# Attention in steps of a pair of heads, planned together with two networks

## The chip, the cores and the metric

One core of one Trainium2 chip runs the whole program. The metric is the device time of one execution in microseconds (us), the median over several. TensorE (PE) multiplies; VectorE (DVE), ScalarE (ACT) and GpSimd (POOL) do the elementwise work; SyncE (SP) issues most DMAs. PE reads its operands from SBUF and writes to PSUM, which has eight banks of 512 fp32 columns.

## What is computed

Attention over 4 batches and 8 heads of 64: 512 local queries see the keys within 32 positions and 32 global keys; 32 global queries see all 544 keys. Its outputs, 4 × 544 rows of 512, go through two networks of width 2048.

```python
def _attn_ref(q_l, k_l, v_l, q_g, k_g, v_g):
    ...
    s_g = scale * np.matmul(q_g, k_all.transpose(0, 1, 3, 2))
    out_g = np.matmul(sm(s_g), v_all)
    ...
    mask = np.abs(pos[:, None] - pos[None, :]) <= window
    s_ll = np.where(mask, s_ll, -1000000000.0)
    s_lg = scale * np.matmul(q_l, k_g.transpose(0, 1, 3, 2))
    a_l = sm(np.concatenate([s_lg, s_ll], axis=-1))
    out_l = np.matmul(a_l, np.concatenate([v_g, v_l], axis=2))
    return np.concatenate([out_g, out_l], axis=2)

def _moe_ref(x, w_in, w_out):
    h = x @ w_in
    return (h * np.cos(h)) @ w_out

def _moe2_ref(x, w_in, w_out):
    h = np.maximum(x @ w_in, 0.0)
    return h * h @ w_out
```

## The kernel before, in words

**Two parts.** Attention comes first and leaves its output, transposed, in `xt`. Then the networks run: each product of a network is made of seven products of half blocks (sums of blocks in, sums of blocks out), in fp32 split into a high and a low part (`split`), in 48 steps. The `ha`, `he`, `hb` products (line 848) are the first layers, `y` (line 940) the second. Weights and x must be split before their products. A planner arranges the networks: each piece of work is an `Op` with a cost on each engine that may do it, with what it needs, and with a latest due time worked back from its users; it places always the piece that can start first, by due time.

**Attention's items.** It runs in 40 items: 32 `Local(p, hb)`, each half of the 512 queries of a pair p of heads, and 8 `Global(b, g)`, each the global queries of four heads. A group is two pairs, so four local items, and one global item; there are eight. A local item does:

- `s_mm` (line 400): scores of four blocks of 64 queries against 160 keys (128 in the window and 32 global), as eight 64 by 64 products; two heads lie in the row halves, two query blocks in the column halves of the array.
- `softmax`: on DVE mask and minimum into `pt`, with the minimum into `st` (line 416), then the exponential on ACT (426). `recip`: sum and reciprocal on DVE (440, 444). `norm`: the global keys' part into `pg` on POOL (449), four blocks of 128 keys, two on DVE (458), two on POOL (463).
- `t_mm` (469, 470): transposes of the probabilities; `t_evac` (475, 479): copies by ACT into `tws` and `tgs`.
- `o_mm`: for each of two query blocks the product of global keys (line 485) at full height, the values `VGZ` padded with zeros to 128 rows, then the window's values (497, `VA` and `VB`, which is `VA` shifted by 64 rows by DMA). `o_evac` copies to `xt` (510).

A global item has the same steps (527 scores, 542 maxima, 551 exponential, 572 normalization, 580 and 583 transposes, 599 values).

**Keys and queries.** `load_k` brings a group's keys so that the 32 global keys stand first: five DMAs a group; the last 32 local keys are left over and are loaded for each batch by themselves (`ktail`). `tr_k` (295) transposes, `k_evac` copies with ACT (308), `k_copy` has POOL make the shifted windows (333) and copies of the global keys for each block (335), and `k_tail` adds the rest. `tr_q` (350) and a copy on DVE (356) do the same for queries.

**Order.** It is written by hand: a table says for each kind of step how many items it lags, and in which order the steps of one round are issued; `BG`, `CB` and `CC` are places in that round where pieces of background (splits of weights and x for the first products) are put by number. Each engine takes its instructions in that order.

```python
CFG = {'order': ['CV', 'LQ', 'S', 'TE', 'BG', 'LK', 'OM', 'TRK', 'KEV', 'CC', 'SM',
           'RC', 'NM', 'CB', 'LV', 'OE', 'TRQ', 'QE', 'KC', 'TM'],
```

Here the minima (`SM`) of an item stand ahead of the reciprocal (`RC`, lag 1) of the item before it. PSUM banks: 0 and 1 transposes, 2 `tg`, 3 to 5 scores, 6 and 7 outputs. After the last item the networks are issued as planned, and `first`, `early` and `late`, the memory of attention, are given up one by one.

## Time and profile before

| what | value |
|---|---|
| time, median of 3 runs | 868.71 us (868.68 to 869.48) |
| the profiled execution: time, span | 867.5 us, 865.7 us |
| PE, DVE, ACT, POOL busy, share of the span | 98%, 75%, 61%, 66% |
| granted PE clock, mean | 1.00 |
| DMA | 182.00 MB, 210 GB/s |

Span is the time between the first and the last instruction of the trace. Busy times count what an engine executes, and not what it issues or waits for. In a timeline the first number is an instruction's start, the second its duration; consecutive instructions of one kind stand in one row with their number, and successive ones overlap, so the distance between starts is what one costs. A product in fp32 leaves two records.

### The profile page before, as it was taken

To read this page: it belongs to the slowest core of one execution; us is meant where nothing else is said; L and a number is where in the kernel's file an instruction comes from. 1 tells how busy PE (TensorE), PEld (TensorE's weight loads), DVE (VectorE), ACT (ScalarE), POOL (GpSimd) and SP (SyncE) were. 2 spreads that over 40 slices of the span, in tenths; PEclk is the share of its full clock that TensorE was granted. 3 is DMA by queue.
4 is the path that set the end of the run, shared out by engine and by line. 5 is a ranking of instruction groups with operands and counts; after the bars stand their busy time and mean duration, and the time that the engine had idled before them with its cause. 6 is when DMAs were issued, how large, how long until landed. Compare 5 with 4: busy or idle time off the path is not lost.

```text
span 865.7 us, 17214 instructions
## 1 busy us (share of the span) xinstructions
PE 847.4 (98%) x6028; PEld 782.1 (90%) x6028; DVE 650.4 (75%) x1521; ACT 529.5 (61%) x1275; POOL 571.1 (66%) x634
## 2 busy tenths in 40 slices
PE   7999999999999999999999999999999999999998
PEld 6777787999999999999999998889988989898886
DVE  7788897999798777967688899896756677454544
ACT  5789787987776666566555777555544554343331
POOL 5479886999797555757377999985635647441221
PEclk9999999999999999999999999999999999999999
DMA  7898865657694578546726646666764677446733
GB/s 165 207 206 183 176 206 185 243 176 247 231 363 154 178 269 312 177 164 266 304 84 227 248 169 240 220 233 237 264 222 140 239 281 231 134 161 246 221 116 84
DMA packets 134262, 182.00 MB, mean 210 GB/s; under 512 B 60960, under 2 KB 114720, under 8 KB 134176
## 3 DMA queue, kind: packets, MB, share of 16 engines
q1 hardware_dynamic: 130736, 179.79, 63.0%
q10 hardware_dynamic: 3440, 1.11, 0.5%
q8 instruction: 48, 0.79, 0.4%
q14 instruction: 38, 0.31, 0.1%
HBM read 141.03 MB, written 35.65 MB: 204 GB/s over the span
## 4 chain that ended last, share of the span: by engine, by line
PE 83%; POOL 4%; DMA 3%; ACT 3%; DVE 2%; SPq 2%; issue 1%; ACTq 0%; POOLq 0%
PE y L940 39%; PE hb L848 15%; PE he L848 10%; PE ha L848 10%; DMA vb<-va 2%; PE s L400 2%; PE o L485 2%; PE o L497 1%; POOL g L172 1%; POOL xs L172 1%; PE tw L469 1%; POOL wf L163 1%; DMA kn<-in_k_l_dram 1%; ACT pt L426 1%; PE tk L295 1%
## 5 line engine op out<-in xcount | busy, mean ns | idle before, releaser
L172 POOL TENSOR_TENSOR g<-cr,g 128x384 fp32r<-128x384 f32 (+1 forms) x192 | 202.6, 1068 | 146.0 <-ACT g L899 141.2
L951 DVE TENSOR_TENSOR xt<-y,xt 128x384 f32<-128x384 f32 (+2 forms) x287 | 170.4, 595 | 96.2 <-PE y L940 94.5
L940 PE MATMUL y<-g,wo 128*128 128x384 f32 (+1 forms) x1152 | 219.2, 327 | 0.4 <-DVE wo L172 0.3
L940 PE MATMUL y<-wo,g 128*128 128x512 f32 x816 | 209.4, 393 | 0.0
L940 PEld LDWEIGHTS y<-g,wo 128*128 128x128 f32 x1152 | 194.1, 188 | 1.5 <-DVE wo L172 0.5
L940 PEld LDWEIGHTS y<-wo,g 128*128 128x128 f32 x816 | 150.0, 188 | 24.1
L848 PE MATMUL hb<-xs,wi 128*128 128x384 f32 (+1 forms) x864 | 166.4, 327 | 1.4 <-ACT cr L888 1.2
L848 PEld LDWEIGHTS hb<-xs,wi 128*128 128x128 f32 x864 | 146.7, 188 | 7.7 <-ACT cr L888 1.6
L848 PE MATMUL he<-xs,wi 128*128 128x384 f32 (+1 forms) x576 | 111.0, 327 | 1.6 <-DVE cr L891 0.8
L848 PE MATMUL ha<-xs,wi 128*128 128x384 f32 (+1 forms) x576 | 110.9, 327 | 0.8 <-DVE cr L891 0.7
L899 ACT ACTIVATE g<-cr 128x384 fp32r<-128x384 f32 (+1 forms) x192 | 93.6, 500 | 20.6 <-DVE cr L891 19.5
L163 POOL TENSOR_TENSOR wf<-wf,cc 128x512 uint32<-128x512 uint32 x64 | 88.3, 1384 | 26.7 <-DVE wf L151 18.6
L848 PEld LDWEIGHTS he<-xs,wi 128*128 128x128 f32 x576 | 98.0, 188 | 6.2 <-DVE cr L891 1.5
L848 PEld LDWEIGHTS ha<-xs,wi 128*128 128x128 f32 x576 | 97.6, 188 | 3.5 <-DVE cr L891 1.0
L885 ACT ACTIVATE cr<-cr,halfpi 128x384 f32<-128x384 f32 (+1 forms) x96 | 55.9, 592 | 11.9 <-DVE cr L880 10.6
L156 DVE SCALAR_TENSOR_TENSOR cc<-raw,cc 128x512 uint32<-128x512 uint32 x64 | 60.9, 958 | 0.0
L426 ACT ACTIVATE pt<-pt,st 128x160 f32<-128x160 f32 x128 | 53.1, 425 | 0.5 <-DVE st L416 0.5
L856 ACT ACTIVATE s<-hb 128x384 f32<-128x384 f32 (+1 forms) x48 | 22.7, 473 | 48.5 <-PE hb L848 48.4
L147 ACT ACTIVATE cc<-raw 128x512 uint32<-128x512 uint32 x64 | 42.5, 670 | 15.9 <-DMA raw<-in_moe_w_in_dram 7.2
L151 DVE TENSOR_SCALAR wf<-wf 128x512 uint32<-128x512 uint32 x64 | 50.0, 785 | 2.7 <-POOL wf L142 1.7
L416 DVE CUSTOM_DVE_ANT_0 pt<-s,mask 128x160 f32<-128x160 f32 x128 | 33.8, 319 | 12.9 <-PE s L400 12.4
L856 ACT ACTIVATE s<-he 128x384 f32<-128x384 f32 (+1 forms) x48 | 22.6, 471 | 32.4 <-PE he L848 32.2
(147 smaller groups left out, 1322.1 us busy)
## 6 DMA issues: line engine op xcount, KB each, us to landing
xs<-xs_T SPq DMA_DIRECT2D x48, 768.0 KB, 5.6
xs<-xs_B SPq DMA_DIRECT2D x36, 768.0 KB, 5.2
raw<-in_moe_w_in_dram SPq DMA_DIRECT2D x32, 512.0 KB, 5.3
raw<-in_moe_w_out_dram SPq DMA_DIRECT2D x32, 512.0 KB, 4.7
xs<-xs_T SPq DMA_DIRECT2D x24, 640.0 KB, 5.6
xs_T<-xs SPq DMA_DIRECT2D x16, 768.0 KB, 4.0
xs<-xs_B SPq DMA_DIRECT2D x18, 640.0 KB, 5.0
xs_B<-xs SPq DMA_DIRECT2D x12, 768.0 KB, 4.8
```

The source lines that it names most:

```text
L147: A.activation(v, raw[q, m, c][:, :, 0].bitcast(U32), AF.Copy, scale=2.0**-29)
L151: V.tensor_scalar(u, u, 3, None, op0=ALU.logical_shift_left)
L156: V.scalar_tensor_tensor(v, t[:, :, 1].bitcast(U32), 0x80000000, v, op0=ALU.bitwise_and, op1=ALU.bitwise_or,)
L163: G.tensor_tensor(u, u, v, op=ALU.add)
L172: eng.tensor_tensor(lo, x, hi.bitcast(F32), op=ALU.subtract)
L426: nc.scalar.activation(self.pt[:, u, :], self.pt[:, u, :], AF.Exp, bias=self.st[:, 0, u : u + 1], scale=-1.0, accum_out=self.st[:, 1, u : ...
L848: nc.tensor.matmul(out, lhsT=w[:, ws, c : c + P], rhs=xs[:, xh, kk, 0:n], start=start and k == 0, stop=k == 5, skip_group_check=True,)
L856: A.activation(self.sb[name], self.hold(bank_name), AF.Copy)
L885: A.activation(self.r[key], self.r[key], AF.Sin, bias=halfpi, scale=TWOPI)
L899: A.activation(GT[s, f][0][:, th * n : th * n + n], self.r[key], AF.Copy)
L940: nc.tensor.matmul(o, lhsT=l, rhs=r, start=k == 0, stop=k == 5)
L951: V.tensor_tensor(dst, y, dst, op=ALU.add)
```

## The change

**Attention in pairs.** `Pair` takes the place of two local items. Its `s_mm` issues sixteen products at once, into banks 2 to 5 (`UNIT` says which unit lies in which bank). Mask, exponential, reciprocal and normalization stay as they are, by half pair (`hb`).

**Global keys' product.** `g_mm` multiplies 64 rows by 64 columns at a time: the upper and the lower row half of the array hold the two query blocks i of a half pair, and the two column halves the values of the two heads h; the result of each i goes to a bank of its own (6 and 7). The values need 64 rows instead of 128, `tgs` holds both half pairs. `v_mm` adds the window's values to both.

```diff
-        def o_mm(self):
-            self.o = bank(BO, "o")[:, 0:256].rearrange("p (i q) -> p i q", i=2)
+                nc.tensor.transpose(self.tw[hb][:, u, :], self.pt[hb][:, u, 0:P], ident)
+
+        def tr_g(self):
+            self.tg = bank(2, "tg")[:, 0 : 2 * P]
+            for hb in range(2):
+                nc.tensor.transpose(self.tg[:, hb * P : hb * P + P], self.pgs[:, hb, :], ident)
+
+        def w_evac(self, hb, eng):
+            copy(eng, self.tws[hb], self.tw[hb])
...
+        def g_mm(self):
+
+
             for i in range(2):
-                for h in range(2):
-                    nc.tensor.matmul(
-                        self.o[64 * h : 64 * h + 64, i, :],
-                        lhsT=VGZ[self.b % 2][:, self.kk, 2 * h + i, :],
-                        rhs=self.tgs,
-                        start=True,
-                        stop=False,
-                        skip_group_check=True,
-                    )
+                self.o[i] = bank(6 + i, "o")[:, 0:256].rearrange("p (k q) -> p k q", k=2)
+            for hb in range(2):
+                for i in range(2):
+                    k = slice(64 * i, 64 * i + 64)
+                    for h in range(2):
+                        d = slice(64 * h, 64 * h + 64)
+                        nc.tensor.matmul(
+                            self.o[i][d, hb, :],
+                            lhsT=VGZ[self.b % 2][k, self.kk, d],
+                            rhs=self.tgs[k, hb, :],
+                            start=hb == 0,
+                            stop=False,
+                            skip_group_check=True,
+                        )
+
+        def v_mm(self, hb):
+            for i in range(2):
                 for half in range(2):
                     v = (VB if half else VA)[self.p // 2 % 2]
                     q = slice(64 * half, 64 * half + 64)
                     for h in range(2):
                         nc.tensor.matmul(
-                            self.o[64 * h : 64 * h + 64, i, q],
-                            lhsT=v[:, 2 * self.hb + i, 2 * (self.p % 2) + h, :],
-                            rhs=self.tws[:, 2 * h + i, q],
+                            self.o[i][64 * h : 64 * h + 64, hb, q],
+                            lhsT=v[:, 2 * hb + i, 2 * (self.p % 2) + h, :],
+                            rhs=self.tws[hb][:, 2 * h + i, q],
                             start=False,
                             stop=True,
                             skip_group_check=True,
                         )
 
-        def o_evac(self):
...
+        def o_evac(self, i, eng):
+            c0 = self.b * SL
+            dst = xt[:, self.kk, c0 : c0 + SL].rearrange("p (k i q) -> p k i q", k=2, i=2)
+            copy(eng, dst[:, :, i, :], self.o[i])
```

**Keys.** They are loaded in whole blocks of 128 local keys; global keys are transposed by themselves, for a batch (`kgT`), and so are global queries. `k_main`, `k_ends`, `k_wins`, `k_glob` and `k_first` fill the windows. `load_k` as it was is gone; keys now come as queries do, by four DMAs a group:

```diff
-    def load_k(gi, h=0, n=4, queues=(nc.sync, nc.sync)):
-        b, g = gi // 2, slice(4 * (gi % 2) + h, 4 * (gi % 2) + h + n)
-        if gi not in kn:
-            kn[gi] = fp.tile([P, 4, 4, D], F32, tag="kn", name="kn", bufs=2)
-        t = kn[gi][:, :, h : h + n]
-        nc.sync.dma_start(t[0:SG, 0], k_g[b, g].rearrange("h p d -> p h d"))
-        nc.sync.dma_start(t[SG:P, 0], k_l[b, g, 0 : P - SG].rearrange("h p d -> p h d"))
-        whole(t, k_l[b, g, P - SG : SL - SG], 1, queues)
```

```diff
+        def k_main(self, eng):
+            src = self.tk[:, SG : SG + 448].rearrange("p (j q) -> p j q", q=64)
+            copy(eng, self.t[:, 1:8, 0:64], src)
...
+        def k_ends(self, eng):
+            t = self.t.rearrange("p j (u q) -> p (j u) q", q=SG)
+            copy(eng, t[:, 1:38:36], self.tk.rearrange("p (u q) -> p u q", q=SG)[:, 0:16:15])
...
+        def k_wins(self, eng):
+            if self.p:
+                copy(eng, self.t[:, 0:7, 64:128], self.t[:, 1:8, 0:64])
...
+        def k_glob(self, eng):
+            src = kgT[:, self.kk, self.b, :]
+            copy(eng, self.t[:, :, P:KTB], src.unsqueeze(1).to_broadcast([P, 8, SG]))
+
+        def k_first(self, eng):
+            copy(eng, self.t[:, 0, 0:SG], kgT[:, self.kk, self.b, :])
...
+            self.s = {k: bank(k, "s") for k in (2, 3, 4, 5)}
+            for hb, i in ((1, 1), (0, 0), (0, 1), (1, 0)):
...
-                    j = 4 * self.hb + 2 * i + half
+                    j = 4 * hb + 2 * i + half
                     for h in range(2):
+                        k, u = UNIT[hb, i, h]
...
                         nc.tensor.matmul(
-                            self.s[h][64 * half : 64 * half + 64, 160 * i : 160 * i + 160],
-                            lhsT=qT[self.p][d, 64 * j : 64 * j + 64],
-                            rhs=kT[self.p][d, j, :],
+                            self.s[k][64 * half : 64 * half + 64, KTB * u : KTB * u + KTB],
+                            lhsT=self.q[d, 64 * j : 64 * j + 64],
+                            rhs=self.t[d, j, :],
```

**One plan.** Attention's steps become `Op`s too: costs on P, A, V, G, and needs such as banks, buffers and loads. `on(n, "AV")` lets the planner choose ACT or DVE for a copy, and normalizations go to POOL or DVE. The order on PE is that of the code (`att_graph`); other engines take attention first and background (splits) into what is left. `close_f`, `close_e`, `close_l` give the memory up when the last transposes of keys and queries, the last users of `ep`, and all of attention are done.

```diff
+    def scores(p):
+        x, r = pairs[p], p % 3
+        main, ends, wins, glob, fst, qe = X[p]
+        kt_free[r] = []
+        s = opP("S", 1.07, x.s_mm, main, ends, wins, glob, qe, *(o for k in s_bank.values() for o in k))
...
+        exps = {0: [], 1: []}
+        for hb, i, h in todo:
+            o = opE({"V": 0.245}, lambda e, a=(hb, i, h): x.top(*a), s, *slots[hb][1])
+            s_bank[UNIT[hb, i, h][0]].append(o)
+            ep_ops.append(o)
+            exps[hb].append(opE({"A": 0.411}, lambda e, a=(hb, i, h): x.exp(*a), o))
+        for hb in range(2):
+            rc = opE({"V": 0.4}, lambda e, hb=hb: x.recip(hb), *exps[hb])
+            x.pg_op[hb] = opE({"G": 0.38}, lambda e, hb=hb: x.norm_g(hb), rc, *fpg)
+            x.n_op[hb] = [
+                opE({"G": 0.34, "V": 0.268}, lambda e, hb=hb, u=u: x.norm(hb, u, e), rc)
+                for u in range(4)
+            ]
```

```diff
+    def outs(p):
+        x, gi = pairs[p], p // 2
+        g = opP("S", 0.427, x.g_mm, x.ge, q_in["vg", x.b], *o_bank[0], *o_bank[1])
...
+        for hb in range(2):
+            o = opP("V", 0.42, lambda hb=hb: x.v_mm(hb), x.we[hb], g, q_in["v", gi], q_in["vb", gi])
...
+        for i in range(2):
+            e = opE(on(256, "AV"), lambda e, i=i: x.o_evac(i, e), o)
...
+        for g in range(NX):
+            scores(2 * g)
+            if g:
+                outs(2 * g - 1)
...
+                g_probs(g - 1)
...
+            if g:
+                g_outs(g - 1)
+                if g + 1 < NX:
...
+            probs(2 * g)
+            if 0 < g < NX - 1:
+                kq(2 * g + 2)
+            g_scores(g)
+            outs(2 * g)
+            probs(2 * g + 1)
```

```diff
+    attention = list(allops)
+    for o in attention:
+        o.att = True
+    close_f = soft(lambda: close(first, "xb"), *fp_ops)
+    close_e = soft(lambda: close(early, "s"), close_f, *ep_ops)
+    close_l = soft(lambda: close(late, "g", "wb"), close_e, *attention)
...
             f = free_at["P"]
+            if adone < len(att_pe):
+                a = att_pe[adone]
+                if missing[a.key]:
+                    a = None
+                if p is None:
+                    return a and (max(f, a.at), a)
+                if a is None or max(f, p.at) + 0.3 < max(f, a.at):
+                    return max(f, p.at), p
+                return max(f, a.at), a
...
-    L = CFG["lag"]
-    for s in range(L["TRK"], NI + L["OE"]):
-        due = lambda k: due_tr.get(s - k)
-        qe = []
-        for c in CFG["order"]:
-            if c in ("BG", "CB", "CC"):
...
-                if c == "S":
-                    i.s_mm()
...
-                elif c == "SM":
-                    for op in i.softmax():
-                        op()
-                elif c == "RC":
-                    for op in i.recip():
-                        op()
-                else:
-                    dict(NM=i.norm, TM=i.t_mm, TE=i.t_evac, OM=i.o_mm, OE=i.o_evac)[c]()
...
-        if s == XBOPEN:
-            first.close()
-            open_pool("xb")
...
+    spin(6)
+    for o in placed:
+        o.fn(o.eng)
```

**The order on PE,** in the middle of attention. Before, a half pair (`tw`, `tg` are transposes of its probabilities, `s` scores, `o` outputs):

```order
L350 MATMUL tq<-ident,qn 128x128 x4
L469 MATMUL tw<-ident,pt 128x128 x4
L470 MATMUL tg<-ident,pg 128x128
L400 MATMUL s<-kT,qT 64x160 x8
L485 MATMUL o<-tgs,vgz_97 64x128 x2
L497 MATMUL o<-tws,va_94 64x64 x2
L497 MATMUL o<-tws,vb_96 64x64 x2
```

After, a pair:

```order
L412 MATMUL tw<-ident,pt_111 128x128 x4
L412 MATMUL tw<-ident,pt_112 128x128 x4
L417 MATMUL tg<-ident,pg_118 128x128 x2
L302 MATMUL tk<-ident,kn 128x128 x4
L309 MATMUL tq<-ident,qn 128x128 x4
L347 MATMUL s<-kT_99,qT_106 64x160 x16
L435 MATMUL o<-tgs_123,vgz_98 64x128 x8
L450 MATMUL o<-tws_119,va_93 64x64 x2
L450 MATMUL o<-tws_119,vb_95 64x64 x2
```

The transposes of two half pairs, of keys and of queries stand together, then all scores of a pair, then its eight global products in a row, and all products with values behind them; one block of each form where there were several.

**The order on DVE,** at a half pair's reciprocal (`L440`, `L444` before, `L383`, `L387` after; `L416` and `L359` are minima, `L458` and `L402` normalizations, `xt<-o` outputs). Before, where `pt,st` of the reciprocal is that of the item before:

```order
L416 ISA pt,st<-s,mask_92 128x160
L416 ISA st 128x1
L440 TENSOR_SCALAR st<-st 128x4
L444 RECIPROCAL st<-st 128x4
L458 TENSOR_SCALAR pt,st<-pt,st 128x128 x2
L172 TENSOR_TENSOR wi<-ws,wi 128x512
L510 COPY xt<-o 128x256
```

After, where `st_113` and `st_114` are the two half pairs whose eight minima have just ended (their last stands first), and `pt_111`, `pt_112` belong to the next pair:

```order
L359 ISA pt_110,st_114<-s,mask_92 128x160
L359 ISA st_114 128x1
L280 COPY xt<-o 128x2x128
L131 SCALAR_TENSOR_TENSOR cc<-raw,cc 128x512 x2
L383 TENSOR_SCALAR st_113<-st_113 128x4
L387 RECIPROCAL st_113<-st_113 128x4
L359 ISA pt_112,st_116<-s,mask_92 128x160
L359 ISA st_116 128x1
L402 TENSOR_SCALAR pt_109,st_113<-pt_109,st_113 128x128 x3
L359 ISA pt_111,st_115<-s,mask_91 128x160
L359 ISA st_115 128x1
L383 TENSOR_SCALAR st_114<-st_114 128x4
L387 RECIPROCAL st_114<-st_114 128x4
```

The reciprocal moved from behind the next item's minima to behind its own, with a copy and two background pieces (`cc`) between for one half pair, and the next pair's minima between for the other.

**The order on POOL,** from the last global normalization (`ptg`) to the first split of a second layer's input (`g`). Before:

```order
L572 TENSOR_SCALAR ptg<-ptg,stg 128x544
L722 TENSOR_TENSOR xr<-xt,xr 128x384 x2
L142 TENSOR_SCALAR wf_2923<-raw 128x512
L163 TENSOR_TENSOR wf_2898<-wf_2898,cc 128x512
L172 TENSOR_TENSOR wo<-wf_2898,wo 128x512
L142 TENSOR_SCALAR wf_3014<-raw 128x512
L172 TENSOR_TENSOR g_3017<-cr,g_3016 128x384
```

After:

```order
L517 TENSOR_SCALAR ptg<-ptg,stg_126 128x544
L637 TENSOR_TENSOR xr<-xt,xr 128x384
L147 TENSOR_TENSOR xs<-xr,xs 128x384
L637 TENSOR_TENSOR xr<-xt,xr 128x384
L138 TENSOR_TENSOR wf_1974<-wf_1974,cc 128x512 x2
L637 TENSOR_TENSOR xr<-xt 128x384
L160 TENSOR_TENSOR ws<-ws,wf_1974 128x256
L147 TENSOR_TENSOR wi<-wf_1974,wi 128x512
L160 TENSOR_TENSOR ws<-wf_1974,ws 128x256
L147 TENSOR_TENSOR wi<-wf_1974,wi 128x256
L637 TENSOR_TENSOR xr<-xt,xr 128x384
L147 TENSOR_TENSOR wi<-ws,wi 128x512
L147 TENSOR_TENSOR g_2723<-cr,g_2722 128x384
```

Twelve pieces stand between instead of six: splits of x (`xr`, `xs`) and of `w_in` (`ws`, `wi`); those of `w_out` (`wo`) no longer stand there.

## Rows read from the trace of the kernel before

**Rows 1.** Busy time by stage: window and length, then each engine, clock, DMA.
```profile
0.00:22.00 22.00, 16.94 (x168) 13.22 (x169) 15.19 (x77) 12.30 (x45) 12.02 (x35) 1.00 0.77 166
22.00:135.40 113.40, 108.70 (x1753) 87.62 (x1753) 96.89 (x534) 96.73 (x362) 89.14 (x160) 1.00 0.81 193
135.40:156.50 21.10, 19.24 (x192) 16.94 (x191) 14.37 (x32) 15.33 (x35) 14.83 (x17) 1.00 0.52 176
156.50:865.70 709.20, 702.50 (x3920) 664.31 (x3918) 523.98 (x880) 405.15 (x838) 455.13 (x423) 1.00 0.61 215
```

**Rows 2.** ACT's timeline, first and last global exponential: start us, duration us, instruction.
```profile
21.98 0.52 ACT L551 ACTIVATE ptg<-sg,stg 128x320 f32<-128x320 f32 x1
...
135.35 0.50 ACT L551 ACTIVATE ptg<-sg,stg 128x320 f32<-128x320 f32 x1
```

**Rows 3.** PE's timeline, the first output product.
```profile
156.53 1.72 PE L940 MATMUL y<-g,wo 128*128 128x384 f32 x9
```

**Rows 4.** PE's timeline through one period of a group.
```profile
106.14 0.77 PE L400 MATMUL s<-kT,qT 64*64 64x160 f32 x14 [0.24 <-ACT ptg L551]
...
109.02 0.77 PE L400 MATMUL s<-kT,qT 64*64 64x160 f32 x16
109.73 0.44 PE L485 MATMUL o<-tgs,vgz 128*64 128x128 f32 x4
110.00 0.28 PE L497 MATMUL o<-tws,va 128*64 128x64 f32 x4
...
110.23 0.39 PE L485 MATMUL o<-tgs,vgz 128*64 128x128 f32 x4
110.45 0.28 PE L497 MATMUL o<-tws,va 128*64 128x64 f32 x4
...
110.78 0.66 PE L580 MATMUL twg<-ident,ptg 128*128 128x128 f32 x4
...
115.07 0.43 PE L362 MATMUL tgq<-ident,qgn 32*128 32x32 f32 x4
115.43 0.66 PE L599 MATMUL og<-tws,va 128*64 128x32 f32 x16
...
121.50 0.48 PE L400 MATMUL s<-kT,qT 64*64 64x160 f32 x2
122.22 0.77 PE L400 MATMUL s<-kT,qT 64*64 64x160 f32 x14 [0.24 <-ACT ptg L551]
```

**Rows 5.** PE's waits until 157 us: us in total, times, longest.
```profile
PE o L497 <- DMA vb<-va: 2.2, 3, 1.5
PE s L400 <- ACT ptg L551: 1.7, 7, 0.3
```

**Rows 6.** DVE's timeline in the same period.
```profile
110.58 0.32 DVE L416 CUSTOM_DVE_ANT_0 pt<-s,mask 128x160 f32<-128x160 f32 x1
...
110.83 0.15 DVE L440 TENSOR_SCALAR_CACHE_REDUCE st<-st 128x4 f32<-128x4 f32 x1
...
111.24 0.35 DVE L458 TENSOR_SCALAR_CACHE_REDUCE pt<-pt,st 128x128 f32<-128x128 f32 x1
...
111.51 0.34 DVE L458 TENSOR_SCALAR_CACHE_REDUCE pt<-pt,st 128x128 f32<-128x128 f32 x1
...
118.84 0.68 DVE L356 COPY qT<-tq 128x512 f32<-128x512 f32 x1
119.44 0.77 DVE L542 TENSOR_REDUCE stg<-sg 128x1 f32<-128x320 f32 x2
120.25 0.21 DVE L547 TENSOR_SCALAR stg<-stg 128x1 f32<-128x1 f32 x1
```

**Rows 7.** Costliest groups, 22 to 135.4 us: count, busy us, mean ns, idle before.
```profile
L426 ACT ACTIVATE pt<-pt,st 128x160 f32<-128x160 f32 x112 | 46.5, 427 | 0.5 <-DVE st L416 0.5
...
L463 POOL TENSOR_SCALAR pt<-pt,st 128x128 f32<-128x128 f32 x54 | 26.5, 500 | 0.0
```

**Rows 8.** POOL's normalizations, 22 to 135.4 us: ns min/median/max, first and last start.
```profile
L463 POOL TENSOR_SCALAR pt<-pt,st x54: 364/371/878, 28.4 to 134.0; 128x128 f32<-128x128 f32 x54
```

927 lines of the change are left out of this document (483 added, 444 removed).

## The prediction

> **What bounds the kernel now.** I read the busy times by stage first [rows 1]. From 156.5 us on PE works 702.50 of 709.20 us, and the change leaves those products alone. The time is to be had before that. Between the first and the last exponential of the global queries [rows 2] lie 113.4 us with seven equal periods of one group each (two pairs of heads and one global item), so 16.2 us a period. In them PE is busy 0.96 of the time, DVE 96.89 us, ACT 96.73, POOL 89.14: no engine is slack. Then 21.1 us pass until the first output product [rows 3], with 1.9 us in which PE idles.
>
> PE's own timeline [rows 4] shows one period: 106.14 to 122.22, 16.08 us. A score item of a half pair occupies 0.71 us (109.02 to 109.73). The output item after it occupies 1.05 us (109.73 to 110.78): global keys' product 0.27 with the change of array form in it, value products 0.23, global 0.22 (110.23 to 110.45), values again, and some 0.1 to leave the form. The four small transposes of global queries or tail keys take 0.36 (115.07 to 115.43). At 121.50 the scores stop after two records until 122.22. The waits [rows 5] say how little PE waits otherwise: 1.7 us in seven periods for the global exponential, 2.2 us for one load of values. So PE sets the period now, with the others close behind.
>
> **The change, PE first.** Four global-key products of a period, two blocks each at 0.22, are 1.76 us. In the new form both heads' column halves and both row halves hold different products, and eight matmuls a pair replace eight at full height. If row halves run side by side as the score products' do, a pair is two steps of 128 columns at 0.22, or 0.88 a period: −0.88. Bounds: 0 if they don't overlap; I take the full gain because scores, the only 64 by 64 form in the rows, do pack that way (eight products of 160 columns in 0.71, where one after the other at the 0.22 for 128 columns they would need 2.2).
>
> Scores: 160 columns at that rate are 0.275 a step; two steps are 0.55, so 0.16 of the 0.71 is the start. One item per pair is then 4 × 0.275 + 0.16 = 1.26, twice 2.52 instead of 4 × 0.71 = 2.84: −0.32 (bounds 0 and −0.64, no start at all). Changes of array form fall from 15 to about 10 a period, at 0.05 to 0.1 each: −0.36 (0 to −0.5). Transposes of tail keys and global queries are 4 sets in the whole run instead of 8, gathered early: −0.2 (0 to −0.36). The stop at 121.50 costs 0.72. Now the score item of the next pair is due only after the global item's outputs, and by these prices 4.9 us of other PE work lies between where 4.1 lay; if that cover is gone the 0.72 stays. Together 16.08 − 0.88 − 0.32 − 0.36 − 0.2 − 0.72 = **13.6 us** a period, 16.1 if every term fails.
>
> **What the other engines then have to do.** I costed the rows of the new order with pitches of DVE [rows 6]: a mask and minimum 0.25 (110.58 to 110.83), the pair around the reciprocal 0.41 (to 111.24), a normalization 0.27 (to 111.51), a copy of 512 columns 0.60 (118.84 to 119.44), the two maxima of a global item 0.81 (to 120.25). The fifth group is the heaviest: 16 minima 3.92 (0.245 each), four reciprocal pairs 1.64, ten normalizations 2.70, the global item 1.26 (0.81 and three tiny ones, 0.45), and the copies 3.38: two of 512 columns, two of 448, three of 256 and one of 64 at 0.60, 0.53, 0.33 and 0.13 (the smaller ones estimated from the 0.60). That is 12.9, and background splitting of weights and x, 2.8, makes 15.7. Counted so, DVE's seven groups are 14.4, 13.4, 12.1, 15.0, 15.6, 14.4, 12.4. ACT, with 16 exponentials at 0.427 [rows 7], the copies and the background, comes to 12.9, 12.2, 13.7, 13.7, 13.2, 12.3, 11.9, and POOL to at most 14.7. ACT and POOL thus lose work (96.73 to 90, 89.14 to 76), as a key block is no longer copied whole and then twice more. DVE keeps its 97.
>
> So PE's 13.6 is not the period any more: the larger of PE and the fullest other engine is 14.4, 13.6, 13.7, 15.0, 15.6, 14.4, 13.6, in sum 100.3. Nothing reaches 1.00: today's fullest engine reaches 0.96 [rows 1]. 100.3 / 0.96 = 104.5 for 113.4: **−8.9 us**.
>
> The Trainium skill says in "TensorEngine Tiling (Array Packing)", section "PSUM Bottleneck", that packing the array speeds up TensorE but not the emptying of PSUM, whose copies may then become the bound. By that rule the saving ends where DVE's copies and minima fill a period, about 14.3 us; by PE's rows alone it would be 13.6. The count above agrees with the rule, and no run has shown it yet.
>
> **Edges.** Startup until 22 us: loads and weight conversion come in another order, and the keys come in whole blocks; no row prices that: I take 0, and ±2 from the 5 us that PE idles there today. The tail: PE's 19.24 us lose one pair's savings, 0.9, and keep 1.9 idle: −0.9 (from −3 if the idle goes, to +4 if x is split late, for POOL has 14.83 us of work there and the new order puts more behind the last global normalization, about 12 us of it instead of 6). After 156.5 nothing. DMAs: four key loads a group on SP's queue instead of five. Two groups' lead hides them; where it fails, a wait like the values' 2.2 [rows 5] is the price, and I leave that wait where it is.
>
> Sum: 867.5 (the profiled execution: its span of 865.7 and 1.8 around it) − 8.9 − 0.9 = 857.7. The median of the three runs, 868.71, stands 1.2 above that execution, which would make 858.9. I say **858.5**.
>
> **Rivals.** *PE alone sets the period.* My count of the others may be pessimistic, since background pieces can slide between groups; the flat mean of DVE is 97 / 7 = 13.9 and not far off. Then 7 × 13.6 = 95.2, −18.2 and −0.9: 848.4. Against it: DVE would be at 1.0.
>
> *Row halves don't overlap.* PE stays at 14.5; groups 14.5, 14.5, 14.5, 15.0, 15.6, 14.5, 14.5 are 103.1, over 0.96 107.4: −6.0 − 0.9 gives 860.6.
>
> *POOL is held up.* A normalization on POOL takes 371 ns at the median and 878 at worst, 500 in the mean [rows 7, 8], so something holds it at times. With six a group at the worst, POOL's 12.7 of today becomes 12.7 + 6 × 0.378 = 15.0, over 0.96 15.6: 109.4, −4.0 − 0.9, 862.6. For it: DVE is denser now. Beside this, the Trainium skill, "SBUF — State Buffer", section "Who interferes with whom", holds that a DVE instruction with two SBUF inputs and a GpSimd one that reads SBUF exclude each other for a whole instruction. The spread from 371 to 878 fits that, but no run here has tried it.
>
> *The gain is lost behind.* The attention ends 9 us sooner, but the splitting of weights and x, a fixed amount on DVE and POOL, doesn't: the first output product then starts where it starts now, at 156.53 [rows 3]. 868, no change. For it: DVE already carries 126.5 us before 156.5. Against it: 30 us of slack there.
>
> *Slower: the reciprocal blocks DVE.* DVE works in order. Today a half pair's reciprocal (110.83) stands behind the minima of the item after it, and did not wait in [rows 6]. In the new order it stands right behind a pair's minima with little between, and at the end of its wait are exponentials on ACT, four of which take 4 × 0.427 [rows 7] after the last minimum has come, with copies queued between them. What stands behind the reciprocal waits too: the next pair's minima, and with them score banks, and PE. There are four reciprocals a period; the break-even is (16.2 − 14.33) / 4 = 0.47 us of idling at each. At 0.6 a period is 14.33 + 2.4 = 16.7, 117.1 in all, +3.7 − 0.9: **870.3**; at 0.85 877. For it: at the place shown the second reciprocal has only two minima and three normalizations, 1.3 us, between it and the first. Against it: that is about what the exponentials need, and two 0.96 us pieces of background stand ahead of the first.
>
> **Chances.** Forecast 0.45; PE alone 0.17; no overlap 0.05; POOL 0.12; lost behind 0.07; reciprocal 0.14. A measurement of this kernel can tell about 0.2%, 1.7 us, from no change. The first four are all faster by more: 0.79. Lost behind is no change, 0.07; the last is slower, 0.14. The range goes from 846 (PE alone, 848.4, with startup's −2) to 869, which takes in the forecast's own ends (−3 and +4 in the tail, ±2 at the start, 853 to 865), POOL and the lost gain, and leaves out the reciprocal and a little below.
>
> **What would show it.** Periods between the global exponentials near 14.9 us, and not 13.6 or 16.7. On PE: eight global products of 128 columns in about 0.44 us; score items near 1.26; no stop like that at 121.50. On DVE: busy above 0.9 in the middle groups, little idle ahead of the reciprocals (over 0.47 each would be the slower rival). On POOL: normalizations near 371 ns. At the end: the first output product some 10 us sooner than 156.53, and the stretch behind it 709 us as before. I am wrong in the price of the rows if the global products take 0.9 a pair, wrong on the bound if DVE is under 0.85 while PE waits, and wrong on the edges if the groups gain 9 us and the total doesn't.

## The result, and the profile after

The changed kernel takes 874.81 us (median of 8 runs, 870.91 to 877.23), the kernel before 869.12 beside it (8 runs, 868.68 to 870.21): a ratio of 1.0063 [1.0045, 1.0081]. It is slower, by some 5.5 us by that ratio, where 858.5 and faster was forecast; the range ended at 869. Each ratio here is to the kernel before, run beside it, and that of experiment 12 leaves out one execution of 2109.46 us.

The profiled execution took 873.76 us, its span is 872.0. Busy time by stage, to be laid beside [rows 1]: window and length, then PE, PEld, DVE, ACT, POOL, granted clock, DMA share, GB/s. The cuts are again the first and the last global exponential and the first output product.

```profile
0.00:24.20 24.20, 19.82 (x183) 15.70 (x184) 14.28 (x88) 13.20 (x46) 10.13 (x33) 1.00 0.92 172
24.20:139.00 114.80, 104.57 (x1740) 82.91 (x1738) 97.32 (x550) 94.20 (x350) 73.90 (x139) 0.96 0.75 185
139.00:162.40 23.40, 18.92 (x167) 16.83 (x166) 21.61 (x36) 17.75 (x38) 21.89 (x20) 0.93 0.44 165
162.40:872.00 709.60, 701.71 (x3920) 663.68 (x3918) 530.14 (x883) 407.81 (x845) 450.72 (x420) 1.00 0.62 215
```

The four lengths before were 21.98 (to the first exponential [rows 2]), 113.37, 21.18 (to the first output product [rows 3]) and 709.17 us. From the starts of the rows below, ACT's timeline of the change, and 162.42 us for its first output product, they are now 24.23, 114.72, 23.47 and 709.58. So of the 6.3 us by which the span grew, **2.25 lie in the startup, 1.35 in the seven periods, 2.29 in the tail** and 0.41 behind (the tail is the stretch from the last global exponential to the first output product). All three stages before the networks are longer than forecast, and the periods by 10.2 us.

```profile
24.23 0.53 ACT L500 ACTIVATE ptg<-sg,stg 128x320 f32<-128x320 f32 x1
...
55.22 0.52 ACT L500 ACTIVATE ptg<-sg,stg 128x320 f32<-128x320 f32 x1
...
76.30 0.52 ACT L500 ACTIVATE ptg<-sg,stg 128x320 f32<-128x320 f32 x1
...
138.95 0.52 ACT L500 ACTIVATE ptg<-sg,stg 128x320 f32<-128x320 f32 x1
```

The rows are the first, third, fourth and last of eight. The seven periods are 15.79, 15.20, **21.08**, 15.48, 17.28, 15.96 and 13.93, where before they were 17.66, 16.65, 16.41, 16.07, 16.71, 16.07 and 13.80. Four are shorter; one, from 55.22 to 76.30, is some 5.7 longer than its neighbours. PE's timeline there (start, duration, instruction, idle before it with what ended it):

```profile
59.46 0.48 PE L347 MATMUL s<-kT,qT 64*64 64x160 f32 x2
63.79 1.58 PE L347 MATMUL s<-kT,qT 64*64 64x160 f32 x30 [3.85 <-ACT tls L278]
65.31 1.07 PE L544 MATMUL og<-tws,va 128*64 128x32 f32 x16
...
68.01 1.97 PE L412 MATMUL tw<-ident,pt 128*128 128x128 f32 x8
...
74.62 1.09 PE L412 MATMUL tw<-ident,pt 128*128 128x128 f32 x8
...
82.58 0.66 PE L544 MATMUL og<-tws,va 128*64 128x32 f32 x16
```

PE stands still for 3.85 us in the middle of a pair's scores, and what it does next takes longer: the same sixteen output products 1.07 at 65.31 and 0.66 at 82.58, the same eight transposes 1.97 and 1.09. It waits for a small copy `tls` on ACT (line 278). ACT's timeline shows that copy at 63.49, behind exponentials, and these behind line 115, the first step in splitting a piece of the weights `w_in`, for whose load ACT waited 5.35 us:

```profile
62.11 0.66 ACT L115 ACTIVATE wf<-raw 128x512 f32<-128x512 f32 x1 [5.35 <-DMA raw<-in_moe_w_in_dram]
62.67 0.41 ACT L372 ACTIVATE pt<-pt,st 128x160 f32<-128x160 f32 x1
...
63.49 0.25 ACT L278 ACTIVATE tls<-tlg 32x128 f32<-32x128 f32 x1
```

SP's queue shows that load as issued at 56.72, behind a group's values (`va`) and the global values (`vgz`), and it landed 5.4 us later:

```profile
52.16 2.61 SPq L240 DMA_DIRECT2D va<-in_v_l_dram  x5
54.81 1.86 SPq L256 DMA_DIRECT2D vgz<-in_v_g_dram  x4
56.72 1.56 SPq L92 DMA_DIRECT2D raw<-in_moe_w_in_dram  x1
```

Before, the first load of `w_in` left 28 us sooner (SP's queue):

```profile
28.67 0.43 SPq L117 DMA_DIRECT2D raw<-in_moe_w_in_dram  x1
```

The chain is thus: SP's queue, a load, ACT in order, a copy for a transposed product's tail, a score bank, PE. The granted clock followed (columns as in the first table, five stretches of 5 us):

```profile
55.00:60.00 5.00, 4.94 (x95) 3.98 (x95) 3.92 (x22) 1.75 (x6) 1.28 (x2) 1.00 0.51 114
60.00:65.00 5.00, 1.21 (x30) 1.08 (x30) 0.76 (x3) 2.89 (x11) 0.00 (x0) 0.97 1.15 246
65.00:70.00 5.00, 5.00 (x56) 4.44 (x51) 3.95 (x32) 4.23 (x20) 1.50 (x4) 0.50 1.25 253
70.00:75.00 5.00, 5.00 (x69) 3.96 (x69) 4.06 (x21) 4.54 (x16) 2.60 (x7) 0.85 0.92 255
75.00:80.00 5.00, 4.97 (x98) 4.24 (x97) 4.48 (x17) 3.40 (x12) 3.75 (x6) 1.00 0.80 186
```

In 60 to 65 PE was busy for 1.21 us, and in the 5 us after that the granted clock was 0.50, which is the 1.2 GHz level; at 75 it was back at 1.00, the 2.4 GHz level. Against a period without background (experiment 4) the stretch from 63.79 to the next pair's scores at 77.05 takes 1.9 us more. 3.85 and 1.9 are the 5.7.

### The profile page after: what moved, and what is told of

Same layout as the page of the kernel before. It is cut to its first block, busy times and chain, and to the rows that moved or that the text cites. A ratio compares the mean times of both kernels' runs of the same rounds, so it can differ in the third digit from the quotient of the medians.

```text
span 872.0 us, 17155 instructions
## 1 busy us (share of the span) xinstructions
PE 845.0 (97%) x6004; PEld 779.1 (89%) x6004; DVE 663.4 (76%) x1555; ACT 533.0 (61%) x1275; POOL 556.6 (64%) x610
## 4 chain that ended last, share of the span: by engine, by line
PE 79%; POOL 8%; DVE 5%; ACT 3%; DMA 3%; issue 2%; SPq 0%; ACTq 0%; DVEq 0%; POOLq 0%
PE y L861 38%; PE hb L769 15%; PE he L769 10%; PE ha L769 9%; POOL xs L147 2%; POOL g L147 2%; PE s L347 1%; DMA raw<-in_moe_w_in_dram 1%; ACT pt L372 1%; PE o L450 1%; PE tw L412 1%; DVE pt L359 1%; POOL wf L138 1%; POOL xr L637 1%; PE sg L478 1%
## 5 line engine op out<-in xcount | busy, mean ns | idle before, releaser
L131 DVE SCALAR_TENSOR_TENSOR cc<-raw,cc 128x512 uint32<-128x512 uint32 x64 | 64.7, 1017 | 0.1
L147 POOL TENSOR_TENSOR wi<-ws,wi 128x512 fp32r<-128x512 f32 x25 | 33.9, 1359 | 27.4 <-ACT wi L171 17.7
```

The lines of the kernel that those rows point to most:

```text
L131: V.scalar_tensor_tensor(v, t[:, :, 1].bitcast(U32), 0x80000000, v, op0=ALU.bitwise_and, op1=ALU.bitwise_or,)
L147: eng.tensor_tensor(lo, x, hi.bitcast(F32), op=ALU.subtract)
```

## The experiments

Theory A: weight loads that land late stand in ACT's and POOL's in-order queues ahead of attention's steps, and that takes the gain. Rivals: the startup without spinning products (B); the new product form on PE (C); the other engines' work in the tail and in the periods (D).

**1. Spins back.** Before, dummy products (`spin`) stand between the first transposes; the change issues its spins all at the start. This puts four back: one after the first global keys' transposes, one after the first `tk`, two after the first `tq`.

```diff
     spin(6)
+    more, n = {0: 1, 1: 1, 2: 2}, 0
     for o in placed:
         o.fn(o.eng)
+        if o.eng == "P":
+            if n in more:
+                spin(more[n])
+            n += 1
```

> The changed kernel with four dummy products more in PE's first microseconds: one behind the global keys' transposes, one behind the first keys', two behind the first queries', as the kernel before had them in other numbers. Nothing else moves. Theory (PE starts at the low clock): in the changed kernel a block of four transposes takes 1.08 us until 16.9 us and 0.66 after it, and the first global exponential comes at 24.2 us where it came at 22.0. With the gaps filled the transposes take 0.66 from about 6 us on, the first exponential comes near 22, and the whole time falls by about 2 us against the changed kernel. Rival (the loads and the longer queue of copies set the start): the blocks are fast but the first exponential stays at 24, and the time within 0.5 us.

PE's timeline at the start, of the change:

```profile
4.97 1.08 PE L302 MATMUL tk<-ident,kn 128*128 128x128 f32 x4 [0.43 <-DMA kn<-in_k_l_dram]
6.41 1.09 PE L309 MATMUL tq<-ident,qn 128*128 128x128 f32 x4 [0.35 <-DMA qn<-in_q_l_dram]
8.23 2.41 PE L347 MATMUL s<-kT,qT 64*64 64x160 f32 x32 [0.73 <-ACT qT L278]
...
16.05 1.05 PE L302 MATMUL tk<-ident,kn 128*128 128x128 f32 x4
16.94 0.60 PE L309 MATMUL tq<-ident,qn 128*128 128x128 f32 x4
```

And of the experiment:

```profile
6.41 0.63 PE L309 MATMUL tq<-ident,qn 128*128 128x128 f32 x4 [0.35 <-ACT kT L278]
...
7.93 1.32 PE L347 MATMUL s<-kT,qT 64*64 64x160 f32 x32 [0.44 <-issue]
```

874.19 us, 1.0054 [1.0032, 1.0075] of before. Four transposes and a pair's scores took 1.09 and 2.41 us without these spins, until 16.9 us, and 0.63 and 1.32 with them; the first global exponential came at 21.07, 3.2 sooner. The total did not move: the third period grew to 22.70, and the wait for the load to 7.4, because the load was issued at 57.01, at its old time. B is a real 3 us, but a wall behind it takes it.

**2. The first piece's conversion later.** The same load, but the first step of that piece's conversion, on ACT, and the one behind it, on DVE, are placed some 7 us later in the plan.

(`CONV` keeps a piece's ops; in 5 its load.)

```diff
+    CONV[0, 0, 0][0].start, CONV[0, 0, 0][2].start = 60.82, 61.75
     placed.sort(key=
```

> The changed kernel with one background piece moved: the first half of the first weights' conversion (one instruction on ACT, the one behind it on DVE) is issued some 7 us later, behind the exponentials that it stood ahead of. Theory (ACT is stopped by a late load): ACT no longer stands 5.35 us for that load, PE's 3.85 us ahead of the scores is gone, and with it the stretch at the lower clock behind it; the third period falls from 21.1 us to about 15.5 and the time by about 5.5. Rival (DVE or the reciprocals are the bound): PE is stopped by something else soon after, the third period stays over 18 and the time falls by less than 2.

872.44 us, 1.0033 [1.0017, 1.0049]. The stop at 59.9 is gone, but ACT then waited 4.60 us for the second piece's load (line 115 at 71.51), and the third period is still 20.13. One wait was taken away, and the next stood behind it.

**3. The global products twice.** The eight products of a pair are issued a second time, into the same place (the first result is overwritten).

```diff
-            for hb in range(2):
+            for hb in (0, 1, 0, 1):
```

> The changed kernel with the global keys' product issued twice, the second overwriting the first: one block of 0.6 us more for each of the 16 pairs, 9.6 us of PE in all, more than what the row halves took away. If PE sets the periods, the time rises by 8 to 10 us against the changed kernel. If DVE and the order of the other engines set them, as the prediction held, most of it goes into PE's waits and the time rises by less than 4.

876.22 us, 1.0060 [1.0039, 1.0080], against 1.0063 for the change: no difference that can be told. In the profiled execution PE's busy time in attention went from 104.57 to 108.98 and the periods from 114.72 to 117.81, with the third one shorter (17.97). By the ratios the whole time shows none of the 4.4 us, so C is not why the total rose. One pair on PE:

```profile
107.20 1.10 PE L435 MATMUL o<-tgs,vgz 64*64 64x128 f32 x32
108.23 0.34 PE L450 MATMUL o<-tws,va 128*64 128x64 f32 x4
```

The sixteen products take 1.03 us between starts, where eight take 0.60 to 0.62 (experiment 4). The second eight thus cost 0.41 to 0.43, and some 0.2 of a pair's 0.62 is the way into this form and out of it.

**4. Attention alone.** No background before 140 us of the plan's time.

```diff
+        if not o.att and not o.soft:
+            o.at = max(o.at, 140.0)
```

> The changed kernel with no background at all in attention: the conversions of weights and the splits of x are planned only after it. The whole time means nothing then (20 to 30 us more); what counts are the periods between the global exponentials. If PE alone sets a bare period they are 13 to 14 us; if a wait of attention's own (the reciprocal behind exponentials, in-order DVE) is there, they stay over 15 without any background.

Everything put off comes later: 891.59 us in its one execution, with a tail of 50.36. What counts are the periods: 15.60, 15.19, 14.89, 14.88, 14.90, 14.88, 12.54, in sum 102.9. One of them by engine, columns as above:

```profile
68.20:83.10 14.90, 14.43 (x251) 11.39 (x250) 12.16 (x77) 12.10 (x49) 6.78 (x17) 1.00 0.71 154
```

PE is busy for 14.43 of 14.90 us, DVE for 12.16. And PE's timeline in it:

```profile
68.94 1.39 PE L347 MATMUL s<-kT,qT 64*64 64x160 f32 x32
70.08 0.69 PE L435 MATMUL o<-tgs,vgz 64*64 64x128 f32 x16
70.70 0.34 PE L450 MATMUL o<-tws,va 128*64 128x64 f32 x4
...
75.32 0.77 PE L412 MATMUL tw<-ident,pt 128*128 128x128 f32 x4
76.29 0.79 PE L412 MATMUL tw<-ident,pt 128*128 128x128 f32 x4 [0.20 <-ACT xt L278]
...
81.40 1.09 PE L412 MATMUL tw<-ident,pt 128*128 128x128 f32 x8
```

So attention by itself takes the 14.9 us a period that were forecast with background in it, and PE sets that period, not DVE. The kernel before was not run without background, so how much of the 1.2 us below its 16.1 is the change's own is not shown; PE's busy time in the seven periods is 99.46 us of 102.88, where before it was 108.70 of 113.40 [rows 1]. From 70.08 to 70.70 a pair's global products take 0.62.

**5. The first two weight loads early,** at 26.4 and 32.75 us of the plan on SP (issued at 32.23 and 39.78 in the trace; in the change at 56.72 and 65.83).

```diff
+    CONV[0, 0, 0].start, CONV[0, 0, 1].start = 26.4, 32.75
     placed.sort(key=
```

> The changed kernel with two DMAs moved on SP's queue and nothing else: the loads of the first two pieces of weights are issued some 30 and 33 us sooner (in the planner's time 26.4 and 32.8 instead of 49.9 and 58.8), where the kernel before had its first one (28.7). Theory (the load comes late in SP's order and in-order ACT stands for it): ACT finds the data there, its wait of 5.35 us and the second one of 4.6 seen when the first piece was moved are both gone, the third period falls from 21.1 us to 15.2 to 15.7, PE's lower clock behind it too, and the time falls by 5 to 6 us against the changed kernel, to about the kernel before. Rival (the DMA engines are full in that stretch and any load is late): another load, of keys or values, comes late instead and the third period stays over 18.

873.41 us, 1.0041 [1.0027, 1.0055]. The third period is 15.31: A holds for that stop. But the fifth is now 21.12. POOL's timeline there, and PE's:

```profile
91.08 0.65 POOL L117 TENSOR_SCALAR wf<-raw 128x512 f32<-128x512 f32 x1 [5.46 <-DMA raw<-in_moe_w_out_dram]
...
92.92 1.15 POOL L517 TENSOR_SCALAR ptg<-ptg,stg 128x544 f32<-128x544 f32 x1
```

```profile
94.13 0.40 PE L528 MATMUL tlg<-ident,ptg 128*32 128x128 f32 x1 [4.70 <-POOL ptg L517]
```

The same fault with `w_out`, on POOL: the global normalization stood behind a load that POOL waited 5.46 us for.

**6. Both of 1 and 5.**

```diff
+    more, n = {0: 1, 1: 1, 2: 2}, 0
...
+    CONV[0, 0, 0].start, CONV[0, 0, 1].start = 26.4, 32.75
```

> Both repairs: the two weight loads early and the four dummy products at the start. By themselves the dummy products brought the first global exponential from 24.2 to 21.1 us and nothing in the whole time, since ACT then stood for the same load 3 us longer. If that load was the wall, the 3 us now show in full: 8 to 9 us below the changed kernel, 2 to 4 below the kernel before. If something else later in attention is a wall (the second stretch of waits near 97 to 106 us, a load of values), the two together give no more than the early loads alone.

874.29 us, 1.0050 [1.0034, 1.0067]; periods 19.58, 15.59, 15.30, 15.49, 21.73, 16.41, 14.95. A start that is 3 us earlier meets other waits: in the first period PE waits three times for loads of queries, 1.6 us in all, and the granted clock of the stretch from 35 to 41 us is 0.72; in the fifth POOL stands 6.2 us for the `w_out` load.

**7. The plan told otherwise:** weight loads of the attention due 70 us sooner, loads of weights and of the networks' x believed to land 4 us behind their transfer and not 2, `LOOK` 0.5 (by how much background gives way to attention's steps on an engine; it was 1.0), and the spins.

```diff
-        return Op({"Q": kb / 330.0}, lambda e: fn(), *needs, lag=2.0)
+        return Op({"Q": kb / 330.0}, lambda e: fn(), *needs, lag=4.0)
...
+    for o in LD:
+        if o.latest < 140.0:
+            o.latest -= 70
...
-    BIAS, LOOK, drift = 6.0, 1.0, [0.0]
+    BIAS, LOOK, drift = 6.0, 0.5, [0.0]
...
```

> The changed kernel with the dummy products and another plan: all weight loads of attention's time are due 70 us sooner and believed to land 2 us later, and background may start up to 0.5 us instead of 1 us before an attention step is due. More of the conversions then lie in attention (in the plan POOL's share of them rises from 28 to 45 us, ACT's from 13.5 to 20, DVE's from 8 to 13). Theory (what is left over the kernel before in the tail, 23.5 us from the last global exponential to the first output product against 21.2, is background put off): the tail falls to 18 to 20 us and the time lies 3 to 6 us below the kernel before. Rival (no engine has room): the periods grow from 15.3 to over 16 by what the tail gives back, and the time equals that of the early loads with the dummy products within 1.5 us.

870.96 us, 1.0014 [1.0002, 1.0026]. Periods between 16.05 and 19.52: background is back in them (POOL 92.29 us busy there, 73.90 in the change), and they are no shorter than those of before. In the longest, the first, POOL still stands 4.11 us for a load of `w_in`.

**8. One number.** Weight loads during attention are believed to land 8 us behind; nothing else.

```diff
+        if not beside[0]:
+            ld.lag = 8.0
```

> The changed kernel with one number of its plan changed: a weight load that is used in attention's time is believed to land 8 us behind its issue instead of 2. The loads keep about their places on SP's queue; the conversions behind them are planned later. Theory (every stop of PE over 3 us in attention is an in-order engine that stands for a weight load which the plan thought landed): no engine waits more than 2 us for such a load, the 3.85 us stop and any that takes its place are gone, PE keeps the full clock from 20 to 130 us, and the seven periods sum to 109 us or less instead of 114.7: about 869 in all. Less background then lies in attention, so the tail is no shorter. Rival (the reciprocal on DVE, or the engines' load): other waits fill the periods, their sum stays above 112.

872.20 us, 1.0022 [1.0008, 1.0037]; the profiled execution, 875.14, is the slowest of its twelve. Without the stop the periods are 15.80, 15.21, 15.72, 15.91, 16.65, 17.83, 14.38, in sum 111.5. One late load is left: in the sixth POOL stands 4.73 us for `w_in`. The tail takes 26.8, and in it DVE is busy for all but 0.12 us:

```profile
24.30:135.80 111.50, 102.94 (x1740) 80.53 (x1739) 93.97 (x540) 91.44 (x345) 71.68 (x140) 0.98 0.78 178
135.80:162.60 26.80, 19.06 (x167) 16.66 (x166) 26.68 (x40) 19.38 (x41) 24.23 (x22) 0.94 0.52 177
```

That is D: in this execution the time won in the groups is asked for again before the first output product.

**9. 8 with loads due 45 us sooner, `LOOK` 0.5 and the spins.**

```diff
+            ld.lag = 8.0
...
+            o.latest -= 45
...
-    BIAS, LOOK, drift = 6.0, 1.0, [0.0]
+    BIAS, LOOK, drift = 6.0, 0.5, [0.0]
...
+    more, n = {0: 1, 1: 1, 2: 2}, 0
...
```

> As the run with 8 us, with the dummy products at the start, the weight loads of attention's time due 45 us sooner, and background allowed up to 0.5 us before an attention step is due. If the three causes are the late loads, the slow start and the background left over for the tail, all three are met: first global exponential near 21, periods summing to 109 to 111, tail 21 to 23, and the whole time 861 to 866, below the kernel before. If SP's queue itself is the limit once attention starts sooner, the first two periods grow over 17 us by waits for keys, queries or values, and the time stays at 867 or more.

875.06 us, 1.0054 [1.0031, 1.0077]: a miss. Periods five and six took 19.44 and 19.26: in the fifth PE waited 2.4 us for the DMA of the shifted values (`vb`), in the sixth POOL 6.1 us for a `w_out` load.

**10. 8, with the splits that become ready at 125 to 150 us left to DVE alone.**

```diff
+        if not o.att and len(o.on) == 2 and "V" in o.on and "G" in o.on and 125.0 < o.at < 150.0:
+            o.on = {"V": o.on["V"]}
```

> As the run with weight loads believed to land 8 us behind, and besides: the background subtractions and sums (operands in SBUF) that DVE or POOL may do and that fall due for either after attention's last steps go to DVE alone; POOL keeps the conversions. In the tail of the 8 us run 14 such pieces of 384 columns took 0.82 us in the mean on DVE and 12 on POOL 1.17, where in attention they took 0.58 and 1.00. Theory (DVE and POOL hold each other up when both read pairs of operands from SBUF, so the leftover work is dear in the tail): DVE's pieces fall back to 0.56 to 0.6, and the tail from 26.8 us to 23 to 25, the time by 2 to 3. Rival (it is plain quantity): DVE alone has 26 pieces at 0.58, 15 us, no less than before; the tail stays at 26 to 29 and the time at that of the 8 us run or above.

874.08 us, 1.0044 [1.0027, 1.0062], no less than 8. Its profiled execution, 871.01, the fastest of six, has the shortest attention with background in it:

```profile
24.20:129.14 104.94, 100.19 (x1740) 78.75 (x1739) 94.24 (x540) 91.41 (x346) 71.89 (x140) 1.00 0.81 188
...
151.56:868.90 717.34, 704.21 (x3919) 665.10 (x3918) 534.01 (x893) 411.35 (x852) 451.13 (x419) 1.00 0.62 214
```

The seven periods sum to 105.0, near the forecast's 104.5, and in them no weight load was waited for more than 1.1 us. The first output product came at 151.56, 5 us sooner than before; what follows then took 717.34 instead of 709.17, with 659 pieces of background in it instead of 640 and stops of PE of 2.63 us at 167.98 and 4.09 us at 261.78. The work left undone was paid for behind.

**11. More background in attention:** 8, with loads due 70 us sooner and `LOOK` 0.

```diff
+            ld.lag = 8.0
...
+            o.latest -= 70
...
-    BIAS, LOOK, drift = 6.0, 1.0, [0.0]
+    BIAS, LOOK, drift = 6.0, 0.0, [0.0]
```

> The 8 us belief with the weight loads due 70 us sooner and no reserve kept for attention's next step, without the dummy products: the most background that the planner will lay into attention (in its plan 45 us on POOL, 15 on DVE, 20 on ACT, against 26, 5.5 and 11 in the 8 us run). If background laid into attention is cheaper there than in the tail, the tail falls from 26.8 to 20 to 22 and the periods grow from 15.9 to at most 16.2, as in the kernel before: 866 to 869 in all. If any background in attention's in-order queues costs PE as much as it saves, periods grow to 16.5 and more and the time stays over 871.

868.29 us, **0.9981 [0.9967, 0.9994]**: with 13 the fastest of all, and some 6.5 us below the change. The granted clock is 1.00 in every stage, and no load in attention was waited for more than 1.7 us:

```profile
22.90:138.74 115.84, 103.82 (x1739) 80.07 (x1738) 104.35 (x545) 99.73 (x362) 91.97 (x157) 1.00 0.84 205
138.74:159.42 20.68, 18.01 (x168) 15.46 (x168) 19.48 (x35) 15.70 (x35) 19.68 (x20) 1.00 0.31 114
159.42:865.40 705.98, 700.67 (x3919) 663.72 (x3918) 521.53 (x877) 401.95 (x832) 440.04 (x412) 1.00 0.62 214
```

The periods are no shorter than before (115.8 in sum): DVE and POOL now do 7 and 18 us more there than in the change. The tail and the stretch behind it gain instead, 0.5 and 3.2 us against before.

**12. 11 with the global products twice** (the second overwrites the first).

```diff
-            for hb in range(2):
+            for hb in (0, 1, 0, 1):
```

> The version with most background in attention (weight loads due 70 us sooner, believed to land 8 us behind, no reserve) and the global keys' product issued twice, the second overwriting the first: 9.6 us more of PE, in a version whose PE nowhere falls to the lower clock and waits for no weight load. If PE sets the periods once the stops are gone, the time rises by 7 to 10 us over that version. If the work of DVE, ACT and POOL until the first output product sets them (periods of 16.5 us there, where attention alone takes 14.9), the time rises by less than 4, and what the row halves save on PE is worth nothing in this place.

869.51 us, 1.0008 [0.9992, 1.0023]. Attention:

```profile
24.96:139.58 114.62, 108.52 (x1963) 86.10 (x1962) 103.56 (x550) 99.81 (x362) 93.53 (x160) 0.99 0.84 207
```

4.7 us more of PE, and the stage is not longer (114.62 for 115.84). By the ratios the whole time rose by some 2 us. With this much background in place PE's time there is nearly free, which fits that shortening it earned nearly nothing.

**13. 11 with the spins.**

```diff
+    more, n = {0: 1, 1: 1, 2: 2}, 0
...
```

> The version with most background in attention and the four dummy products at the start. In the changed kernel the dummies brought the first global exponential 3.2 us forward and a weight load took it all back. With that load out of the way: 2 to 3 us less than without them, 865 to 866.5, if the engines' work or PE sets the periods behind; no gain if keys, queries and values then come late on SP's queue (first period over 18 us instead of 16.9).

868.22 us, 0.9981 [0.9970, 0.9991]: as 11. The first exponential came 1.6 us sooner, the first and fourth periods were longer (18.21 and 19.06 for 16.87 and 17.21).

## Why the prediction was wrong

**The price on PE was half right.** Forecast 16.08 to 13.6 us a period, measured bare (experiment 4, without background) 14.9. Between starts, before and in experiment 4, without the marked waits (0.24 us then, 0.43 now): scores with the stop at 121.50 [rows 4] 3.31 to 2.39, so −0.92 for the −1.04, and that stop is gone; global products 1.91 to 1.22, so −0.69 for −0.88. Row halves do overlap, and the eight products themselves cost the forecast's 0.44 (experiment 3: 0.41 to 0.43); what makes a pair 0.62 is the way into the form and out of it, and the 0.36 for fewer changes of form came to 0.09. What I had not priced: the window and key transposes cost 0.92 more (`tw` 1.76 to 2.32, `tk` and `tq` 1.96 to 2.32). They now stand in a row. Eight `tw` take 1.59 us where they follow their normalizations one by one (75.32 to 76.91; three of the second four run on DVE from 75.79, 76.06 and 76.33, 0.34 each), against 0.93 where all but the last are done before (81.40 to 82.33), and `tq` at 78.02 waits for the copy of `tw` out of its bank. The small transposes went further than forecast (−0.36 for −0.2); `og` (−0.14), `tg` (−0.16) and `sg` (+0.10) were not in the sum.

**The bound was read wrong.** Of the change, DVE is busy for 97.32 of 114.80 us, the 97 I counted, but that is 0.85, my own sign of a wrong bound. "Reaches 0.96" was PE's share; I gave it to DVE. Bare, PE reaches 0.97 with DVE at 0.82; with background in, experiment 11, DVE and PE both reach 0.90 and no engine more. The Trainium skill's rule in "TensorEngine Tiling (Array Packing)", section "PSUM Bottleneck", is that the emptying of PSUM may become the new limit. Experiment 4 speaks against it for attention by itself (PE 14.43 of 14.90, DVE 12.16), and experiment 12 fits a wider form of it, in which splits count as much as copies.

**The step that failed first** is "DMAs: … Two groups' lead hides them … I leave that wait where it is". I counted key loads, and not the weight loads that the plan sends through the same queue: the first leaves 28 us later than before, and its conversion stands on ACT where the plan, with 1.6 us for the transfer and 2 behind it, believes the load landed; it took 5.4. That is 5.7 us in the third period, at a place that none of my rivals named. Experiments 5, 6 and 8 show it by taking it away, 1 and 2 by moving it. Of the other 4.5 us that the periods lie above the forecast some 4 are spread over the other six, 15.6 in the mean for 14.9; the longest, 17.28, has a granted clock of 0.86 from 97 to 109 us. What each of the six lost was not taken apart.

**The edges were the second.** Startup "0, and ±2": it was +2.25. I priced nothing for the spins that the change leaves out, and they explain all of it: in fourteen profiled executions the first exponential came at 22.52 to 24.96 without them and at 20.83 to 21.83 with them. On balance their removal costs nothing, since later waits absorb it (1, 13). The tail was forecast at −0.9 and came to +2.29, inside the +4 I gave for "if x is split late"; that is what happened. Attention is placed first. Counted in the traces by the lines of the splitting steps of x and weights, the seven periods hold 85 pieces of background on ACT, DVE and POOL before and 64 in the change, the tail 25 and 43. (POOL's 73.90 us in the periods for 89.14 is mostly attention's own work that has left POOL, as the forecast counted; background is 3.3 us of the difference.) So the tail is full: DVE 21.61 and POOL 21.89 of 23.40 us, and PE waits in a first layer's product for a copy on ACT, ahead of which ACT had waited 2.32 us for POOL's `ws`:

```profile
152.68 1.68 PE L769 MATMUL hb<-xs,wi 128*128 128x384 f32 x6 [4.07 <-ACT s L777]
```

**The rival "the gain is lost behind" came nearest in its mechanism,** with a chance of 0.07. With 53 pieces among the groups the periods are shorter, and the gain is asked for again in the tail (8) or, against that rival and my "after 156.5 nothing", behind a first output product that does come sooner (10). With 98 pieces there (7, 11) the periods are no shorter than before. As far as these runs go, the fixed amount of splitting sets the end: the best version is 0.2% below before, the limit of what can be told. No run put the 85 pieces of before among the groups, so how much of the gain is left at equal background is not shown.

**Refuted:** the reciprocal that blocks DVE, my slower case. DVE's wait before it, in the seven periods (in total, times, longest): 

```profile
DVE st L383 <- ACT pt L372: 2.8, 5, 1.1
```

That is 2.8 us in 28 reciprocals, where 0.47 each would have been 13. Refuted too is POOL held up at normalizations, 371 to 878 ns before [rows 7, 8]: all 45 (ns min/median/max, first and last start) now take the same:

```profile
L407 POOL TENSOR_SCALAR pt<-pt,st x45: 366/372/374, 31.6 to 138.1; 128x128 f32<-128x128 f32 x45
```

**What spread is left.** Runs of the change differ by 6.3 us, those of before by 1.5 beside it and by 2.6 to 4.2 beside the experiments. A load whose landing varies would do that; it was not tried.

## What to carry to other kernels

A plan that mixes background with a critical chain on in-order engines must be told when its loads land, or the cheapest conversion becomes a stop for everything behind it. Before pricing what a shorter chain gives, ask where the work that fills its gaps will go: where a fixed amount of it has to be done before a later stage, the gain in the chain is only lent. Compare stage marks of the two traces (here first and last exponential, first output product): a stage that grew by 1 us here held a gain of 4 and a loss of 6.

## What was not expected of the hardware

**The clock after a stop.** After 3.85 us without work PE was granted 0.50 of its clock in the next 5 us and 0.85 in the 5 after; that cost half as much again as the stop.

**A slow start that the clock's row doesn't show.** Until 16.9 us four transposes lasted 1.05 to 1.11, as long as after the stop (1.06 at 70.20), while the granted clock of the startup reads 1.00. Four dummy products between the first transposes removed it from 6 us on. That 1.00 rests on no record: the trace's first record of the granted clock is at 16.91 us in the change and at 5.42 in experiment 1, and four transposes take 1.05 at 16.05 and 0.60 at 16.94. That the clock was at its lower level before is read from these durations; it is not recorded.

**Two engines on SBUF.** A difference of 128 x 384 on DVE takes 0.54 to 0.58 us, but 1.62 where POOL is in two of its own. DVE's timeline in the tail of the change, then POOL's:

```profile
145.15 1.62 DVE L637 TENSOR_TENSOR xr<-xt 128x384 f32<-128x384 f32 x1 [0.78 <-POOL xr L637]
...
148.73 0.54 DVE L637 TENSOR_TENSOR xr<-xt 128x384 f32<-128x384 f32 x1
```

```profile
145.08 2.83 POOL L138 TENSOR_TENSOR wf<-wf,cc 128x512 uint32<-128x512 uint32 x2
148.95 1.18 POOL L637 TENSOR_TENSOR xr<-xt 128x384 f32<-128x384 f32 x1 [1.03 <-ACT cc L122]
```

At 148.73 POOL had stopped at 147.91, and DVE is back at 0.54. The Trainium skill, "SBUF — State Buffer", section "Who interferes with whom", says that such instructions exclude each other, and these rows agree. It made the tail dearer than its pieces. Leaving them to DVE alone (10) took the tail from 26.8 to 22.4, but with 38 pieces in it instead of 48, so what the exclusion alone costs is not shown.
